# One set of rows for the sums of squares, one fixed zeroed tile of probabilities, and another buffer for a block's third result tile

## The chip, the cores and the metric

The kernel runs on one core of a Trainium2 chip. The metric is device microseconds of one execution. A core has five engines with queues of their own: TensorE (PE, matmuls), VectorE (DVE), ScalarE (ACT), GpSimd (POOL) and SyncE (SP), which here only issues transfers. The engines wait for each other by semaphores; an instruction that has to wait holds up all that stands behind it in its queue.

## The reference

Three layers in a row, on 4 x 576 = 2304 tokens of 512 features, in float32. The first is attention with 8 heads of 64; four heads look at a window of 32 keys, four at every fourth of 128. The second is a gated layer with a norm ahead of it, the third a layer with a PReLU.

```
mask_plain = (rel >= 0) & (rel < window)                                        # heads 0..3
mask_dil = (rel >= 0) & (rel < window * dilation) & (rel % dilation == 0)       # heads 4..7
attn = softmax(where(mask, scale * q @ k.T, -1e9)) @ v            # 4 x 8 x 576 x 64
x = attn as 2304 x 512
xn = x / sqrt(mean(x * x) + 1e-06) * rms_g
g = xn @ w_gate;  x = (g * sigmoid(g) * (xn @ w_val)) @ w_out     # 512 -> 1536 -> 512
h = x @ w_in;  out = (max(h, 0) + alpha * min(h, 0)) @ w_out      # 512 -> 2048 -> 512
```

## The kernel before

Every value that goes into a matmul is split into two float16 numbers, a high and a low part, and a product takes three matmuls (high-high, high-low, low-high). So most values are made twice: ACT writes the high part with a scale, DVE or POOL subtracts it from the value and writes the low part.

The tokens go through the two wide layers in seven blocks: 256, 256, 384, 384, 384, 256 and 384 tokens (blocks 0 to 6). A block has a phase A (`mm1`, `mm2`: the gated layer, closed by `y_out`) and a phase B (`mm3`, `mm4`: the PReLU layer, closed by `o_out`). Blocks 4 to 6 do phase B in a tail of their own. Each phase runs over chunks of 128 hidden features, and each chunk is a slot: the matmuls of the chunk, on ACT a Tanh (L921) or a Relu (L985) that evacuates PSUM, on DVE a second step (L922, L986), on ACT the high half (L925, L988), on POOL the low half (L931), and two slots later the matmuls that add the chunk to the result in PSUM (`acc`).

The attention is cut into groups of up to 96 queries x 128 keys x 4 heads. Its steps stand in a list, and between two slots some are taken from it, at a pace that has each block's tokens ready in time; each is given a high priority. The first groups use a path with float32 matmuls; the last 33 of them (the later path, some 224 to 690 us) use functions whose names begin with `a_`:

- `a_load` brings q into a tile `rq` and k and v into `rkv` (two buffers each), on SP's queue.
- `a_max` lets ACT square q, k and v (L511, three instructions) and add them up by row into `ams`. Of `ams` there were two sets, by `i % 2`, for each of three numbers of query rows (96, 64, 32).
- `a_split_hi` takes a ones matmul over these rows (`psw<-ams,ones`), DVE makes scales `sc` of it, and ACT writes the high halves of q, k and v (L537, L539, L540); `a_split_lo` adds the low halves.
- `a_turn_qk` transposes q and k by a transfer (L561, SP's queue) into `qkT`.
- `a_score` has the score matmuls, the softmax (four exponentials on ACT, L587), and writes the high half of the probabilities into `phl` (L700). Where a group has fewer than 128 keys, POOL first zeroes the other columns (L699). `a_prob` adds the low half (L706, POOL).
- `a_turn_p` transposes `phl` by a transfer (L712) into `pT`; `a_value` has the matmuls with v; `weigh` divides, by way of a tile `xd` of the tag `st` for dilated groups (L602 on ACT, L603 on DVE), and writes to DRAM.

Group i's steps are spread over neighbouring steps of the list: `a_max` of i stands in the list before the split of i, and the split of i - 1 before the `a_max` of i.

`o_tile` copies 128 tokens of a block's result out of PSUM into a tile `o` (L1003) and sends it out from ACT's queue (L1008). A block of 384 tokens has three. The tag `st` has two buffers, and `xd` uses it as well. The tag `hl2` has two buffers and holds the split rows: `yhl` of `y_out`, and `xhl` of the attention's norm.

The order of the instructions on each engine is not that of the code alone: the framework's scheduler orders them by dependencies, priorities and its own estimate of times. So a change of a buffer moves instructions elsewhere.

Of the kernel before, what the change touches and what calls it, by code (L numbers as in the profile page):

```python
# [8 lines left out]
F32 = mybir.dt.float32  # L9
F16 = mybir.dt.float16  # L10
# [19 lines left out]
def kernel(  # L30
# [14 lines left out]
    nc = tc.nc  # L45
    B, H, S, D = q.shape
    DM = H * D
# [3 lines left out]
    HH = H // 2  # L51
# [9 lines left out]
    wk = ctx.enter_context(tc.tile_pool(name="wk", bufs=1))  # L61
    dram = ctx.enter_context(tc.tile_pool(name="dram", bufs=1, space=DRAM))
    at_stack, ps_stack = ctx.enter_context(ExitStack()), ctx.enter_context(ExitStack())
    at = at_stack.enter_context(tc.tile_pool(name="at", bufs=1))
# [25 lines left out]
    vhl = [at.tile([128, HH, 2, D], F16, tag=f"vhl{i}", name=f"vhl{i}") for i in range(NV)]  # L90
    vh, vl = ([t[:, :, a] for t in vhl] for a in range(2))
    ams = const.tile([128, 3, 2, 3], F32, name="ams")
    scratch = dram.tile([B * S, HH * D], F32, name="scratch")

    def mm(o, a, b, start, stop):
        nc.tensor.matmul(o, a, b, start=start, stop=stop)  # L96

    def psw():
        return ps_w.tile([128, 512], F32, tag="w", name="psw")
# [17 lines left out]
    def band(m, rows, cols, c0, lo, hi, off=0, fill=-NEG):  # L117

        view = m[0:rows, c0:c0 + cols]
        nc.gpsimd.affine_select(  # L120
            out=view, in_=view, compare_op=ALU.is_ge, fill=fill,
            base=off - lo, pattern=[[1, cols]], channel_multiplier=-1,
        )
        nc.gpsimd.affine_select(
            out=view, in_=view, compare_op=ALU.is_ge, fill=fill,
            base=hi - off, pattern=[[-1, cols]], channel_multiplier=1,
        )

    def constants():
        nc.vector.memset(ident, 0.0)  # L130
        nc.gpsimd.affine_select(
            out=ident, in_=ident, compare_op=ALU.not_equal, fill=1.0,
            base=0, pattern=[[-1, 128]], channel_multiplier=1,
        )
        nc.vector.memset(ones_1, 1.0)
        nc.vector.memset(eps, 1e-30)
        nc.gpsimd.memset(qkhl, 0.0)
        nc.gpsimd.memset(ams, 0.0)
        nc.vector.memset(mhalf, -0.5)
        nc.vector.memset(m_spp, 0.0)  # L140
        for m in (m_norm, m_tail):
            nc.vector.memset(m, -BIG)
        band(m_spp, 128, 128, 0, -31, 0, fill=-BIG)

        et = wk.tile([4, 32, 4], BF16, tag="st", bufs=2, name="et")
        nc.vector.memset(et, 0.0)
        nc.gpsimd.affine_select(
            out=et, in_=et, compare_op=ALU.not_equal, fill=1.0,
            base=0, pattern=[[0, 32], [-1, 4]], channel_multiplier=1,
        )  # L150
        same = psw()[:, 0:128]
        mm(same, et.rearrange("p a c -> p (a c)"), et.rearrange("p a c -> p (a c)"), True, True)
        nc.vector.tensor_scalar(m_spd, same, BIG, -BIG, ALU.mult, ALU.add)
        band(m_spd, 128, 128, 0, -127, 0, fill=-BIG)
        band(m_norm, 96, 128, 0, 1, 32)
        for r in range(2):
            view = m_tail[:, 48 * r:48 * r + 48]
            band(m_tail, 32, 48, 48 * r, 1, 32, 16 * r)
            nc.gpsimd.affine_select(
                out=view, in_=view, compare_op=ALU.is_ge, fill=-NEG,  # L160
                base=-16 if r else 15, pattern=[[0, 48]], channel_multiplier=1 if r else -1,
            )
# [342 lines left out]
    def a_max(i):  # L505
        g = groups[i]
        nq, nk = g["nq"], g["nk"]
        am = ams[:, {96: 0, 64: 1, 32: 2}[nq], i % 2]
        junk = wk.tile([128, 512], BF16, tag="junk", bufs=1, name="junk")[:, 0:HH * D]
        for n, c, src in ((nq, 0, g["rq"][:nq]), (nk, 1, g["rkv"][:nk, 0]), (nk, 2, g["rkv"][:nk, 1])):  # L510
            nc.scalar.activation(  # L511
                junk[:n], src.rearrange("p h d -> p (h d)"), ACTF.Square, accum_out=am[:n, c:c + 1])
        g["am"] = am
# [49 lines left out]
    def softmax(g, scores, scale, masked=False):  # L563

        nq, nk = g["nq"], g["nk"]
        s = g["s"]
        sv = s[:nq, :, :nk]
        for ps, hs in () if masked else scores:
            n = len(range(HH)[hs])
            nc.vector.scalar_tensor_tensor(  # L570
                s[:nq, hs, :nk], ps[:nq, :, :nk], scale,
                g["mask"][:nq, :nk].unsqueeze(1).to_broadcast([nq, n, nk]), ALU.mult, ALU.max)
        mx = at.tile([128, 2, HH], F32, tag="mx", bufs=4, name="mx")
        if masked:
            for ps, hs in scores:
                nc.vector.tensor_reduce(mx[:nq, 0, hs], ps[:nq, :, :nk], axis=AX.X, op=ALU.max)
            nc.vector.tensor_scalar(mx[:nq, 1], mx[:nq, 0], -scale, None, ALU.mult)
        else:
            nc.vector.tensor_reduce(mx[:nq, 1], sv, axis=AX.X, op=ALU.min)  # L579
        g["dn"] = at.tile([128, HH, 1], F32, tag="dn", bufs=4, name="dn")  # L580
        for ps, hs in scores if masked else ():
            for n, h in enumerate(range(HH)[hs]):
                nc.scalar.activation(
                    s[:nq, h, :nk], ps[:nq, n, :nk], ACTF.Exp, bias=mx[:nq, 1, h:h + 1], scale=scale,
                    accum_out=g["dn"][:nq, h])
        for h in () if masked else range(HH):
            nc.scalar.activation(  # L587
                s[:nq, h, :nk], s[:nq, h, :nk], ACTF.Exp, bias=mx[:nq, 1, h:h + 1], scale=-1.0, accum_out=g["dn"][:nq, h])
# [96 lines left out]
    def a_score(i):  # L685
        g = groups[i]
        nq, nk = g["nq"], g["nk"]
        qT, kT = g["qT"], g["kT"]
        ps = psw().rearrange("p (h c) -> p h c", h=HH)
        for h in range(HH):  # L690
            mm(ps[:nq, h, :nk], qT[:, 2 * h, :nq], kT[:, h, :nk], True, False)
            mm(ps[:nq, h, :nk], qT[:, 2 * h + 1, :nq], kT[:, h, :nk], False, True)
        g["s"] = at.tile([128, HH, 128], F32, tag="s", name="s")
        softmax(g, [(ps, slice(0, HH))], g["sc"][:nq, 6:7])
        sv = g["s"][:nq, :, :nk]
        phl = at.tile([128, 2, HH, 128], F16, tag="phl", name="phl")
        g["phl"] = phl
        if nk < 128:
            nc.gpsimd.memset(phl[:nq, :, :, nk:128], 0.0)  # L699
        nc.scalar.activation(phl[:nq, 0, :, :nk], sv, ACTF.Copy)  # L700

    def a_prob(i):
# [121 lines left out]
    def score(i):  # L824
        a_score(i)
        a_prob(i)
# [9 lines left out]
    def second_half(i):  # L836
        some((score, i - 2), (a_turn_qk, i - 1), (a_max, i))
        if i < NG:
            next_load(i)
# [156 lines left out]
    def o_out(j):  # L996
        rc = ysc.pop(j)
        for n in range(ncols(j) // 128):
            o_tile(j, n, acc[n], rc[:, n:n + 1])

    def o_tile(j, n, src, rc, eng=nc.scalar):
        o = wk.tile([128, DM], F32, tag="st", bufs=2, name="o")
        nc.scalar.activation(o, src, ACTF.Copy, scale=rc)  # L1003
        col = 0
        for t0, m in blocks[j][0]:
            a, e = max(col, n * 128), min(col + m, (n + 1) * 128)
            if a < e:
                eng.dma_start(  # L1008
                    out=out[t0 + a - col:t0 + e - col, :], in_=o[a - n * 128:e - n * 128, :])
            col += m  # L1010
# [106 lines left out]
    def out_t(t):  # L1117
        p = tail["acc"]
        tl = tail["tl"]
        m1 = tl.tile([128, 1, 256], F32, tag="m1", bufs=1, name="m1o")  # L1120
        nc.scalar.activation(m1[:, 0], p[3][:, 0], ACTF.Copy)

        y = tl.tile([128, 7, 256], F32, tag="yb", bufs=1, name="yo")
        nc.vector.tensor_tensor(y[:, 0:5:4], p[0][:, 0:2], m1.to_broadcast([128, 2, 256]), ALU.add)
        nc.vector.tensor_tensor(y[:, 6], p[2][:, 0], y[:, 4], ALU.add)
        nc.vector.tensor_tensor(y[:, 2:4], p[1][:, 0:2], y[:, 6:7].to_broadcast([128, 2, 256]), ALU.add)
        nc.vector.tensor_tensor(y[:, 5], p[1][:, 1], y[:, 4], ALU.add)
        nc.vector.tensor_tensor(y[:, 1], p[2][:, 1], y[:, 5], ALU.add)
        yv = y.rearrange("p a c -> p (a c)")
        for n in (1, 0):  # L1130
            i = 2 * t + n
            o_tile(*tiles[i], yv[:, n * 512:(n + 1) * 512], rct[:, i:i + 1], nc.sync if n else nc.scalar)
# [120 lines left out]
    fill()  # L1253
    nc.sync.dma_start(out=al, in_=alpha.rearrange("(c p) -> p c", p=128))
    constants()

    first = max(n for n, s in enumerate(steps) if s[1] == 0) + 1
# [104 lines left out]
```

## Time and profile before

| | before |
|---|---|
| median of three runs | 974.19 us (973.42 to 974.59) |
| the profiled execution | 973.93 us, span 972.1 us |
| PE busy | 912.4 us (94% of the span) |
| DVE busy | 675.2 us (69%) |
| ACT busy | 550.4 us (57%) |
| POOL busy | 324.2 us (33%) |
| granted TensorE clock, mean | 0.974 |

The span runs from the first instruction to the last; 1.8 us of the profiled execution lie around it. Busy times are sums over the whole span, and the engines work at the same time: what counts is where the engine that ends last had to wait.

### The profile page before, as it was taken

How to read it: one execution, taken by the hardware profiler on the slowest of the kernel's cores; microseconds unless marked ns; L12 is line 12 of the kernel's file. 1: busy time of each engine (PE TensorE's matmuls, PEld its weight loads, DVE VectorE, ACT ScalarE, POOL GpSimd, SP SyncE). 2: the span in 40 equal slices, each digit the busy share in tenths (PEclk: the TensorE clock that was granted, in tenths of full speed). 3: DMA queues.
4: the chain of work that ended last, by engine and by line, in shares of the span. 5: the costliest groups of instructions: out<-in, count | busy, mean ns of one | idle time of the engine just before them, and what ended most of it. 6: DMA issues, size and time to landing. Idle time of an engine off the chain costs nothing.

```text
span 972.1 us, 18834 instructions
## 1 busy us (share of the span) xinstructions
PE 912.4 (94%) x6760; PEld 618.8 (64%) x6760; DVE 675.2 (69%) x1602; ACT 550.4 (57%) x1537; POOL 324.2 (33%) x333
## 2 busy tenths in 40 slices
PE   6559899999998999998999999999999999999997
PEld 3547667865555666554555554555775557889986
DVE  5999897998878666565565775545554836777674
ACT  3426587756899866666655776544434324344342
POOL 2313341231444544332232233323253622322221
PEclk9678899999999999999999999999999999999999
DMA  9992356455236455544435554232311002000000
GB/s 264 326 353 85 94 167 168 136 165 142 52 62 95 97 101 83 106 84 89 101 75 83 107 105 85 47 80 53 45 23 22 1 1 34 1 23 23 2 24 22
DMA packets 191614, 88.15 MB, mean 91 GB/s; under 512 B 176800, under 2 KB 180384, under 8 KB 191520
## 3 DMA queue, kind: packets, MB, share of 16 engines
q1 hardware_dynamic: 189504, 83.27, 37.4%
q10 hardware_dynamic: 2016, 3.67, 1.1%
q8 instruction: 53, 0.87, 0.4%
q14 instruction: 41, 0.34, 0.1%
HBM read 55.32 MB, written 6.55 MB: 64 GB/s over the span
## 4 chain that ended last, share of the span: by engine, by line
PE 54%; DVE 15%; DMA 11%; ACT 9%; issue 7%; POOL 2%; SPq 1%; ACTq 0%; DVEq 0%; POOLq 0%
PE psw L96 24%; PE p L96 15%; PE acc L96 14%; ACT s L587 2%; DMA rkv<-in_v_dram 2%; DMA rkv<-in_k_dram 2%; DVE wb L230 2%; DVE wb L231 2%; DMA wb<-in_moe_w_out_dram 2%; DMA rq<-in_q_dram 2%; DVE wb L407 1%; DVE wb L229 1%; ACT junk L511 1%; ACT wb L402 1%; DVE t L922 1%
## 5 line engine op out<-in xcount | busy, mean ns | idle before, releaser
L96 PEld LDWEIGHTS <-wb 128*128 128x128 f16 (+1 forms) x4866 | 454.0, 99 | 203.6 <-DVE wb L231 17.9
L96 PE MATMUL psw<-xyall,wb 128*128 128x384 f16 (+1 forms) x2784 | 431.2, 305 | 4.4 <-DVE xd L603 1.5
L96 PE MATMUL acc<-wb,hlall 128*128 128x512 f16 x822 | 198.7, 380 | 5.6 <-ACT hlall L988 2.3
L96 PEld LDWEIGHTS <-hlall 128*128 128x128 f16 x822 | 78.7, 98 | 89.3 <-POOL hlall L931 5.4
L931 POOL TENSOR_TENSOR hlall<-t,hlall 128x384 f16<-128x384 f32 (+1 forms) x58 | 59.3, 1022 | 160.3 <-ACT hlall L925 142.0
L96 PE MATMUL acc<-wb 128*128 128x512 f16 (+1 forms) x402 | 83.6, 353 | 18.7 <-DVE wb L231 15.5
L96 PE MATMUL p<-xyall,wb 128*128 128x256 f16 (+1 forms) x960 | 88.7, 251 | 0.0
L1096 POOL TENSOR_TENSOR wb<-fa,wb 128x640 f16<-128x640 f32 x32 | 45.4, 1421 | 111.8 <-ACT wb L1095 111.8
L922 DVE SCALAR_TENSOR_TENSOR t<-t,psw 128x384 f32<-128x384 f32 (+1 forms) x84 | 41.0, 489 | 53.0 <-ACT t L921 53.0
L96 PE MATMUL p<-wb 128*128 128x256 f16 x672 | 77.6, 273 | 0.3 <-DVE yhl L966 0.3
L921 ACT ACTIVATE t<-psw,tsc 128x384 f32<-128x384 f32 (+1 forms) x84 | 44.0, 524 | 40.9 <-PE psw L96 39.1
L587 ACT ACTIVATE s<-s,mx 96x128 f32<-96x128 f32 (+2 forms) x132 | 50.0, 380 | 15.3 <-DVE mx L579 13.8
L931 POOL TENSOR_TENSOR hlall<-p,hlall 128x256 f16<-128x256 f32 (+1 forms) x49 | 39.8, 814 | 56.3 <-ACT hlall L988 45.1
L986 DVE SCALAR_TENSOR_TENSOR p<-m,oma,psw 128x256 f32<-128x256 f32 (+1 forms) x64 | 34.5, 538 | 31.3 <-ACT m L985 30.9
L1094 DVE SCALAR_TENSOR_TENSOR wb<-fa,wb 128x384 f16<-128x384 f32 x32 | 40.5, 1269 | 22.2 <-ACT wb L1093 22.1
L402 ACT ACTIVATE wb<-wb,wsg 128x512 f16<-128x512 f32 x68 | 46.1, 711 | 16.8 <-DVE wsg L339 10.2
L706 POOL TENSOR_TENSOR phl<-s,phl 96x512 f16<-96x512 f32 (+2 forms) x33 | 36.0, 1090 | 58.4 <-ACT phl L700 50.5
L1095 ACT ACTIVATE wb<-fa 128x640 f16<-128x640 f32 x32 | 23.5, 735 | 55.9 <-DVE fa L1088 55.9
L405 POOL TENSOR_TENSOR wb<-wb 128x512 f16<-128x512 f32 x28 | 38.2, 1371 | 39.9 <-ACT wb L404 20.9
L231 DVE SCALAR_TENSOR_TENSOR wb<-wb 128x512 int32<-128x512 int32 (+1 forms) x56 | 49.8, 891 | 0.2
L594 DVE TENSOR_SCALAR dn<-dn 96x4 f32<-96x4 f32 (+3 forms) x52 | 8.4, 162 | 58.9 <-ACT s L587 53.7
L931 POOL TENSOR_TENSOR wb<-t,wb 128x256 f16<-128x256 f32 (+1 forms) x26 | 27.4, 1055 | 63.5 <-ACT wb L925 63.5
(202 smaller groups left out, 1383.3 us busy)
## 6 DMA issues: line engine op xcount, KB each, us to landing
wb<-in_moe_w_out_dram SPq DMA_DIRECT2D x28, 512.0 KB, 4.4
wb<-in_moe_w_in_dram SPq DMA_DIRECT2D x16, 512.0 KB, 3.8
wb<-in_moe_w_gate_dram SPq DMA_DIRECT2D x12, 512.0 KB, 6.7
wb<-in_moe_w_val_dram SPq DMA_DIRECT2D x12, 512.0 KB, 6.9
out_dram<-o ACTq DMA_DIRECT2D x14, 256.0 KB, 3.8
rkv<-in_k_dram SPq DMA_DIRECT2D x23, 128.0 KB, 2.5
rkv<-in_v_dram SPq DMA_DIRECT2D x23, 128.0 KB, 3.0
rq<-in_q_dram SPq DMA_DIRECT2D x23, 96.0 KB, 2.0
```

What stands on the lines that cost most here:

```text
L96: nc.tensor.matmul(o, a, b, start=start, stop=stop)
L231: nc.vector.scalar_tensor_tensor(w, r[:, :, :, 0], 29, w, ALU.logical_shift_right, ALU.bitwise_or)
L402: nc.scalar.activation(half(b, 0), dec(b), ACTF.Copy, scale=wsg[:, s:s + 1])
L405: nc.gpsimd.tensor_tensor(half(b, 1), dec(b), half(b, 0), ALU.subtract)
L587: nc.scalar.activation(s[:nq, h, :nk], s[:nq, h, :nk], ACTF.Exp, bias=mx[:nq, 1, h:h + 1], scale=-1.0, accum_out=g["dn"][:nq, h])
L706: nc.gpsimd.tensor_tensor(phl[:nq, 1, :, :nk], g["s"][:nq, :, :nk], phl[:nq, 0, :, :nk], ALU.subtract)
L921: nc.scalar.activation(t[:, :T], pg[:, :T], ACTF.Tanh, scale=tsc[:, chunk(c):chunk(c) + 1])
L922: nc.vector.scalar_tensor_tensor(t[:, :T], t[:, :T], 1.0, pg[:, :T], ALU.add, ALU.mult)
L931: nc.gpsimd.tensor_tensor(a[:, 1, :T], t[:, :T], a[:, 0, :T], ALU.subtract)
L986: nc.vector.scalar_tensor_tensor(p[:, :T], m[:, :T], oma[:, c:c + 1], ps[:, :T], ALU.mult, ALU.add)
L1094: nc.vector.scalar_tensor_tensor(l[:, 0:3], f[:, 0:3], 0.25, h[:, 0:3], ALU.mult, ALU.subtract)
L1096: nc.gpsimd.tensor_tensor(l[:, 3:8], f[:, 3:8], h[:, 3:8], ALU.subtract)
```

## The change

Three edits. The rows for the sums of squares have one set instead of two. The tile of probabilities `phl` is one tile for all groups, zeroed once at the start by POOL, instead of one allocated for each group with the unused columns zeroed each time. The third result tile of a block takes a buffer of the tag `hl2` instead of `st`.

```diff
+    phl = at.tile([128, 2, HH, 128], F16, tag="phl", name="phl")
...
         nc.gpsimd.memset(ams, 0.0)
+        nc.gpsimd.memset(phl, 0.0)
...
-        am = ams[:, {96: 0, 64: 1, 32: 2}[nq], i % 2]
+        am = ams[:, {96: 0, 64: 1, 32: 2}[nq], 0]
...
-        phl = at.tile([128, 2, HH, 128], F16, tag="phl", name="phl")
         g["phl"] = phl
-        if nk < 128:
-            nc.gpsimd.memset(phl[:nq, :, :, nk:128], 0.0)
         nc.scalar.activation(phl[:nq, 0, :, :nk], sv, ACTF.Copy)
...
     def o_tile(j, n, src, rc, eng=nc.scalar):
-        o = wk.tile([128, DM], F32, tag="st", bufs=2, name="o")
+        o = wk.tile([128, DM], F32, tag="hl2" if n == 2 else "st", bufs=2, name="o")
```

With the added lines the line numbers shift: L511 becomes L513, L537, L539 and L540 become L539, L541 and L542, L587 becomes L589, L602 becomes L604; behind `a_score` they are one lower (L700 becomes L699, L985 L984, L988 L987, L1003 L1002, L1008 L1007).

The instructions also change their order. On ACT, in block 2's phase B, the squares of one group (96 query rows) stood ahead of the exponentials of the group two before it; this is the place in the trace around 450 to 455 us. `wb` is a chunk's high half, `m` the Relu's result. Before:

```order
L988 ACTIVATE wb<-p 128x384
L511 ACTIVATE junk,ams<-rq 96x256
L511 ACTIVATE junk,ams<-rkv 128x256 x2
L587 ACTIVATE s,dn<-s,mx 96x128 x4
L985 ACTIVATE m<-psw 128x384
L700 ACTIVATE phl<-s 96x512
L988 ACTIVATE wb<-p 128x384
L537 ACTIVATE qkhl<-rq,sc 96x4x2x64
L539 ACTIVATE qkhl<-rkv,sc 128x4x64
L540 ACTIVATE vhl_86<-rkv,sc 128x4x64
```

The same place on ACT in the changed kernel:

```order
L987 ACTIVATE wb<-p 128x384
L589 ACTIVATE s,dn<-s,mx 96x128 x4
L984 ACTIVATE m<-psw 128x384
L699 ACTIVATE phl<-s 96x512
L513 ACTIVATE junk,ams<-rq 96x256
L987 ACTIVATE wb<-p 128x384
L513 ACTIVATE junk,ams<-rkv 128x256
L539 ACTIVATE qkhl<-rq,sc 96x4x2x64
L541 ACTIVATE qkhl<-rkv,sc 128x4x64
L542 ACTIVATE vhl_86<-rkv,sc 128x4x64
L513 ACTIVATE junk,ams<-rkv 128x256
```

The three squares have moved behind the exponentials, the Relu and the copy of the probabilities, to both sides of the split copies of the group before them.

The second place on ACT is the end of block 2, where its three result tiles are copied, around 463 to 470 us. Before:

```order
L921 ACTIVATE t<-psw,tsc 128x384
L1003 ACTIVATE o<-acc,rc 128x512 x2
L1008 DMA out_dram<-o 128x512
L587 ACTIVATE s,dn<-s,mx 96x128 x4
L1008 DMA out_dram<-o 128x512
L1003 ACTIVATE o<-acc,rc 128x512
L700 ACTIVATE phl<-s 96x512
L1008 DMA out_dram<-o 128x512
L602 ACTIVATE xd<-psw 32x256
```

And in the changed kernel:

```order
L920 ACTIVATE t<-psw,tsc 128x384
L1002 ACTIVATE o<-acc,rc 128x512 x2
L1007 DMA out_dram<-o 128x512
L589 ACTIVATE s,dn<-s,mx 96x128 x4
L1007 DMA out_dram<-o 128x512
L1002 ACTIVATE o<-acc,rc 128x512
L604 ACTIVATE xd<-psw 32x256
L699 ACTIVATE phl<-s 96x512
L1007 DMA out_dram<-o 128x512
```

The copy into `xd` has moved ahead of the copy of the probabilities and now comes right behind the third result tile.

The third place is on SP's queue, around 558 to 562 us, where the loads of one group and the transpose of q and k of another leave. Before:

```order
L608 DMA scratch<-xd 96x256
L499 DMA rq<-in_q_dram 96x4x64
L501 DMA rkv<-in_k_dram 128x4x64
L561 DMA_TRANSPOSE qkT<-qkhl 128x12x96
L503 DMA rkv<-in_v_dram 128x4x64
```

And in the changed kernel:

```order
L610 DMA scratch<-xd 96x256
L501 DMA rq<-in_q_dram 96x4x64
L503 DMA rkv<-in_k_dram 128x4x64
L505 DMA rkv<-in_v_dram 128x4x64
L563 DMA_TRANSPOSE qkT<-qkhl 128x12x96
```

The load of v has passed the transpose.

## Rows read from the trace of the kernel before

**Rows 1.** Busy time by stretch: PE, PEld, DVE, ACT, POOL; granted clock, DMA share, GB/s.

```profile
200.00:640.00 440.00, 422.42 (x2794) 248.52 (x2793) 298.74 (x763) 307.79 (x928) 159.98 (x172) 1.00 0.47 92
640.00:960.00 320.00, 319.74 (x2657) 239.86 (x2655) 197.16 (x446) 126.47 (x261) 107.18 (x96) 1.00 0.12 23
```

**Rows 2.** Line 511, the squares: ns min/median/max; idle time before them (us, times).

```profile
L511 ACT ACTIVATE junk<-rkv x66: 398/416/418, 224.2 to 636.9; 128x256 bf16<-128x256 f32 x46, 96x256 bf16<-96x256 f32 x20
...
  DMA rkv<-in_k_dram: 21.3, 19
  DMA rq<-in_q_dram: 21.1, 21
  DMA rkv<-in_v_dram: 7.0, 10
```

**Rows 3.** PE's timeline: start, us, instruction, idle before it and its releaser.

```profile
337.02 1.04 PE L96 MATMUL acc<-wb,hlall 128*128 128x512 f16 x4 [0.59 <-ACT hlall L988]
...
455.17 1.04 PE L96 MATMUL acc<-wb 128*128 128x512 f16 x4 [1.09 <-ACT wb L988]
...
496.82 0.97 PE L96 MATMUL psw<-xyall,wb 128*128 128x384 f16 x5 [0.34 <-DVE t L922]
...
531.76 0.44 PE L96 MATMUL psw<-qkT 128*96 128x128 f16 x5 [1.79 <-DVE t L922]
...
540.68 0.60 PE L96 MATMUL acc<-wb 128*128 128x512 f16 x2 [0.69 <-ACT wb L925]
...
572.31 0.52 PE L96 MATMUL psw<-vhl,pT 96*32 96x128 f16 x8 [0.54 <-DMA pT<-phl]
...
601.58 0.61 PE L96 MATMUL acc<-wb 128*128 128x512 f16 x2 [1.44 <-ACT wb L988]
```

**Rows 4.** ACT's timeline: two squares that waited for their load.

```profile
494.79 0.42 ACT L511 ACTIVATE junk<-rkv 128x256 bf16<-128x256 f32 x1 [0.81 <-DMA rkv<-in_v_dram]
...
530.14 0.42 ACT L511 ACTIVATE junk<-rkv 96x256 bf16<-96x256 f32 x1 [2.61 <-DMA rkv<-in_v_dram]
```

**Rows 5.** ACT's timeline: the copy that PE stood for at 455.17.

```profile
454.59 0.52 ACT L988 ACTIVATE wb<-p 128x384 f16<-128x384 f32 x1 [0.32 <-DVE p L986]
```

**Rows 6.** ACT's and PE's timelines: a third square, its read, the group's ones matmul.

```profile
574.03 0.40 ACT L511 ACTIVATE junk<-rkv 96x256 bf16<-96x256 f32 x1
574.33 0.19 ACT L511 ACTIVATION_READ_ACCUMULATOR junk<-rkv 96x1 f32 x1
...
578.49 0.18 PE L96 MATMUL psw<-ams,ones 96*128 96x3 bf16 x1
```

**Rows 7.** Line 503, issue of a v load; line 561, who waited for its transposes.

```profile
L503 SPq DMA_DIRECT2D rkv<-in_v_dram x39: 421/498/1776, 123.7 to 634.1; - x39
...
  PEld L96: 1.2, 2
  PE psw L96: 0.5, 1
```

**Rows 8.** ACT's and PE's timelines at the result tiles of block 2.

```profile
463.51 1.26 ACT L1003 ACTIVATE o<-acc,rc 128x512 f32<-128x512 f32 x2
...
468.42 0.69 ACT L1003 ACTIVATE o<-acc,rc 128x512 f32<-128x512 f32 x1 [1.95 <-DMA out_dram<-o]
...
469.52 0.37 ACT L602 ACTIVATE xd<-psw 32x256 f32<-32x256 f32 x1
...
470.39 2.11 PE L96 MATMUL psw<-xyall,wb 128*128 128x384 f16 x12 [1.47 <-DVE xd L603]
...
473.28 0.63 ACT L736 ACTIVATE xhl<-x 96x512 f32<-96x512 f32 x1 [2.25 <-DVE x L605]
```

**Rows 9.** Line 699, the memsets; their waits (us, times); line 137 by form.

```profile
L699 POOL MEMSET phl<- x10: 301/302/309, 298.7 to 689.6; 32x256 f16 x6, 64x256 f16 x4
...
  DMA pT<-phl: 22.7, 9
...
L137 POOL MEMSET qkhl<- 128x1536 f16 x1 | 1.4, 1377 | 0.3 <-POOLq L1340 0.3
```

## The prediction

> **What bounds the kernel now.** The first view is the table of stretches [rows 1]. From 200 to 640 us TensorE (PE) is busy 422.42 of 440 us at full granted clock; from 640 to 960 it is busy 319.74 of 320. So PE is the bound, and 17.6 us of holes between 200 and 640 are all that can be won after 200 us. Before 200 us the program keeps its order on every engine, but for one memset on POOL at the start. The later attention path, which the change touches, runs between 224 and 690 us.
>
> The second view is what the squares of `a_max` waited for [rows 2]. ScalarE (ACT) runs 99 of them (three for each of 33 groups) at 416 ns in the median, and stood 21.3, 21.1 and 7.0 us ahead of them until k, q or v had landed: 49.4 us. ACT has much idle time, so this costs only where something that PE needs stands behind a square on ACT's queue.
>
> The third view, PE's timeline, decides that. I took every hole of 0.3 us or more between 200 and 640 and followed it back: from the instruction that released PE to what that one waited for, until a wait for a load came or none was left. In seven places the way ends at a square that stood for its load [rows 3]; an eighth, at 292, begins at one too but has other waits on its way, and is left out. Two of these squares show the pattern [rows 4]: the one at 494.79 waited 0.81 us for v, the one at 530.14 waited 2.61. Behind it on ACT stand an evacuation of PSUM or the exponentials, then comes DVE, then PE's hole, 1 to 4 us later. The hole can be longer or shorter than the wait, since other work lies between.
>
> **The change, part by part.**
>
> *One set of rows.* With `i % 2` the squares of group i may run before the ones matmul of group i-1 has read its own row maxima; with index 0 they may not, if both have the same number of query rows. Nothing is computed more or less: 99 squares before and after. But the scheduler now puts them behind that matmul. Counting the other instructions ahead of each on ACT, 23 of the 33 groups have their first square 3 to 23 instructions later (10 in the median), most now close ahead of the split copies of the group before; nine stand where they stood, within one, and one comes earlier. The first place in the order on ACT shows it: before, the squares stood ahead of the exponentials of another group; now those run first. Ten instructions of at least the length of a square are 10 x 0.42 = 4.2 us that the load has more, an estimate from [rows 2], against single waits of 0.81 and 2.61 us [rows 4], so most of the waits go.
>
> Which holes close? Of the seven in [rows 3], five go back to a square that is moved: 0.59 (337.02), 1.09 (455.17), 0.34 (496.82), 0.69 (540.68) and 0.54 (572.31), together 3.25 us. The other two, 1.79 (531.76) and 1.44 (601.58), go back to groups that keep their place (the square at 530.14 is of one), and stay. Something else is late next where a hole closes: at 455.17 the copy L988 that releases PE had itself waited 0.32 us for DVE [rows 5], a third of that hole. I count a quarter of the 3.25 as coming back: -3.25 + 0.8 = -2.45 us.
>
> What it adds is a wait of the squares for the ones matmul, and behind them on ACT the copies that PE wants. The way from a square to the ones matmul of its own group tells how much room there is. The shortest among the moved groups is that of the group whose third square starts at 574.03 and whose matmul runs at 578.49 [rows 6]: 578.49 - 574.03 - 0.40 - 0.19 for the read of the sum = 3.9 us. Three squares take 3 x 0.416 = 1.2 us plus three such reads, 1.8 us in all, and the split copies have to wait for the scales from DVE anyway, so the squares fill time in which ACT would stand. Cost taken: 0; bound above: the rival below.
>
> The Trainium skill (Trainium Kernel Development and Optimization, Best Practices) says "Double-buffer for performance: Overlap DMA with compute". By that rule giving up the second set loses overlap, and the time would go up. The trace doesn't bear it out: what is doubled here is not the target of a transfer, and the second set only let ACT stand for loads sooner.
>
> *The order on SP.* The transposes of q and k (L561) leave from the same queue as the loads. Counting the loads ahead of each of the 33: seven have one or two more ahead of them now, two have one fewer. The order on SP shows one place: the v load passes the transpose. A v load holds the queue 0.50 us [rows 7], so at most 7 x 0.5 = 3.5 us if each transpose were waited for, and 0 if none. PE and its weight loads waited for such a transpose three times in 33 [rows 7]: 7 x 3/33 x 0.5 = 0.3 us. I take +0.3. The gain on the other side (the v load 1.5 us sooner, as long as a transpose holds the queue) is part of a rival.
>
> *The third result tile.* At 463.51 two copies of block 2's results fill both buffers of tag `st`; the third copy waits until the first transfer out has landed, and runs at 468.42 after 1.95 us of idle. Behind it stands `xd`, at 469.52, and PE, which had stood for it, goes on at 470.39 after 1.47 us [rows 8]. With its own buffer the third copy runs at once. But the next user of `st` is then `xd`, which waits for the same transfer: it can start where the copy started, at 468.42. Gain 469.52 - 468.42 = 1.10 us of the 1.47. Its bounds are 0 (if `xd` is late for another reason) and 1.47. The buffer taken from `hl2` is next wanted by an `xhl`; the first after it, at 473.28, takes the other buffer and waits for DVE anyway [rows 8]: 0. The other block with three tiles, block 3, ends past 640 us, where PE is full [rows 1], as it is at the two third tiles of the tail: 0.
>
> *The fixed zeroed tile.* Ten memsets of 0.30 us go from GpSimd (POOL), and with them 22.7 us in nine waits for the transpose before [rows 9]. No hole of PE goes back to one, and the longest waits lie past 640 us, where PE is full: 0. The low half of the probabilities, which POOL makes next, waits for the same transpose either way. The new memset at the start is 128 x 1024; the nearest row is 128 x 1536 in 1.38 us [rows 9], so about 0.92 us on POOL in the first microseconds, where PE waits for the q and k loads. 0, at most +0.9.
>
> **Sum.** -2.45 + 0.3 - 1.10 = -3.25 us against the profiled 973.93, that is 970.7. The median of the three runs is 0.26 above the profiled one; with it 970.9 us. About 0.2% (1.95 us) is what measurement can tell from no change, so this is faster by more than that, 0.33%, not by much.
>
> **Rivals.**
>
> *The wait changes owner.* The squares stand for the ones matmul instead of the load, and holes of the same size open at other places; the change then does only the 1.10: 973.1 us, no change by the bound. For it: the order of 23 groups shifts, and a hole's origin moves easily. Against it: 3.9 us of room where 1.8 are needed.
>
> *PE stands for the late squares: slower.* Where ACT reaches the squares late, the ones matmul, which stands in PE's queue among the large matmuls, waits, and PE with it. The mean of the seven holes is 6.48 / 7 = 0.93 us. Against the sum of -3.25, 3.25 / 0.93 = 3.5 such holes cancel the gain, and (3.25 + 1.95) / 0.93 = 5.6 make the kernel slower by 0.2%; one in every third of the 23 moved groups, seven, gives 970.9 + 7 x 0.93 = 977.4 us. Against it: no wait of PE for a square stands among the holes before. For it: the squares now come at the last place where they are in time.
>
> *The unmoved holes close too: faster still.* The sooner v loads and the shorter ACT queue ahead also shorten the waits of 1.79 and 1.44 us [rows 3], and nothing comes back: 973.93 - 3.25 - 3.23 - 1.10 + 0.26 = 966.6 us.
>
> **How the numbers follow.** Forecast as reckoned 0.48; unmoved holes too 0.14; owner changes 0.26; slower 0.12. So faster 0.62, same 0.26, slower 0.12. The likeliest case alone spans 969.5 to 972.5: all five holes, 1.47 for the tile and 0 for SP, 973.93 - 3.25 - 1.47 + 0.26; or half of them, 1.10 and 1 us for SP, 973.93 - 1.63 - 1.10 + 1.0 + 0.26. For 8 in 10 the range takes in the rival at 966.6 and of the slower one the part near no change: 966.6 to 976.0.
>
> **What would show it.** Right: ACT's idle time ahead of the squares falls from 49.4 us to about 10; PE's busy time from 200 to 640 stays 422 while that stretch's work ends about 3 us sooner, with the five holes gone; ahead of the third result tile no wait, `xd` behind it waits about 2 us for the transfer out; the memsets of the probabilities gone and nothing else changed by it; PE's holes before 200 us as they were. Wrong: PE waits for a square ahead of the ones matmul, or new holes of 0.5 us and more behind the transposes of q and k.

## The result and the profile after

The changed kernel takes 958.78 us in the median of four runs (957.45 to 959.12), against 974.39 (973.42 to 975.72) for the one before: ratio 0.9836, 95% interval 0.9819 to 0.9853. That is 15.6 us, almost five times the forecast of 3.25, and outside the range. The profiled execution has a span of 956.9 us.

The busy time by stretch of the changed kernel, in the columns of [rows 1]:

```profile
200.00:640.00 440.00, 433.28 (x2890) 257.90 (x2888) 299.38 (x784) 313.69 (x949) 159.95 (x169) 1.00 0.48 95
640.00:940.00 300.00, 300.00 (x2529) 227.81 (x2527) 185.34 (x419) 117.12 (x238) 101.78 (x89) 1.00 0.11 20
```

PE now stands 6.7 us of the 440, not 17.6; past 640 us it is full, as before. What the squares waited for (line 513 now):

```profile
its engine sat idle before it (us, times) until:
  DMA rq<-in_q_dram: 5.7, 6
  DMA rkv<-in_k_dram: 4.3, 3
  DMA rkv<-in_v_dram: 2.9, 3
  PE psw L97: 0.3, 1
```

So 12.9 us of load waits are left of the 49.4 in [rows 2], in 12 places instead of 50; the wait for the ones matmul, which takes their place, is 0.3 us in one.

PE's timeline, all holes of at least 0.2 us that are left between 255 and 680 us:

```profile
292.08 1.25 PE L97 MATMUL acc<-wb,hlall 128*128 128x512 f16 x5 [1.10 <-ACT hlall L924]
...
300.41 0.55 PE L97 MATMUL psw<-vhl,pT 128*96 128x128 f16 x8 [1.51 <-DVE sg L340]
...
342.96 0.82 PE L97 MATMUL acc<-wb,hlall 128*128 128x512 f16 x3 [0.56 <-ACT hlall L987]
...
547.14 0.59 PE L97 MATMUL psw<-vhl,pT 128*96 128x128 f16 x8 [0.45 <-DMA pT<-phl]
```

The kernel before had 21 such holes in this stretch, 14.7 us together. The third of the four that are left, 0.56 us at 342.96, stands where the kernel before had none. All seven of [rows 3] are closed, the two of groups that keep their place among them. At one of these two groups ACT still waits for its loads, as its timeline shows:

```profile
507.92 0.42 ACT L513 ACTIVATE junk<-rq 32x256 bf16<-32x256 f32 x1 [0.85 <-DMA rq<-in_q_dram]
...
511.38 0.42 ACT L513 ACTIVATE junk<-rkv 96x256 bf16<-96x256 f32 x1 [2.50 <-DMA rkv<-in_k_dram]
...
515.61 0.42 ACT L513 ACTIVATE junk<-rkv 96x256 bf16<-96x256 f32 x1 [1.24 <-DMA rkv<-in_v_dram]
```

These are the squares of the group that had the wait of 2.61 us in [rows 4]: 4.6 us of waits stand here, and no hole of PE follows.

The third result tile of block 2, on ACT:

```profile
457.72 0.67 ACT L1002 ACTIVATE o<-acc,rc 128x512 f32<-128x512 f32 x1
458.88 0.37 ACT L604 ACTIVATE xd<-psw 32x256 f32<-32x256 f32 x1 [0.50 <-DMA out_dram<-o]
```

The copy runs at once, and `xd` behind it waits 0.50 us for the transfer out.

Where the 15.2 us between the two profiled executions come from, by stage: I paired the 3,744 matmuls that read `xyall` (each one's place in the order of its kind is the same in both) and took the difference of their start times. At 47 us the changed kernel is 2.4 us behind, at 245 us 1.3. Between 245 and 257 us 1.7 come back, which is the clock: from 240 to 250 us the execution before had a granted clock of 0.83, this one 1.00. From 257 to 605 us it goes from 0.4 ahead to 14.8; past that only 0.4 is added. So 14.4 us come from the stretch of the later attention path: 3.0 of them up to 450 us, 4.9 between 450 and 473, 1.1 between 473 and 504, 3.0 between 525 and 548, and 2.3 between 548 and 605.

Not all of the 14.4 can be put down to the change. The hole of 1.47 us at the third result tile is 0.45 us at most in the profiles of the kernels below, and those of 0.28 us at 479 and of 0.34 at 497 behind it are in none; together they are 2.1 us. In the execution before, the first transfer out (issued at 464.22) landed after 4.11 us. In the profiles with the second edit alone, with one group moved and with three, which change little or nothing of the order up to there, it landed after 2.0 to 2.4 us, and the third copy didn't wait for it. With one group moved that copy is

```profile
465.12 0.67 ACT L1003 ACTIVATE o<-acc,rc 128x512 f32<-128x512 f32 x1
```

Why the transfer took longer in that one execution is not shown.

### The profile page after: what moved, and what is told of

Same layout as the page of the kernel before. It is cut to its first block, busy times and chain, and to the rows that moved or that the text cites. A ratio compares the mean times of both kernels' runs of the same rounds, so it can differ in the third digit from the quotient of the medians.

```text
span 956.9 us, 18827 instructions
## 1 busy us (share of the span) xinstructions
PE 906.7 (95%) x6760; PEld 619.6 (65%) x6760; DVE 666.4 (70%) x1602; ACT 548.2 (57%) x1537; POOL 321.2 (34%) x324
## 4 chain that ended last, share of the span: by engine, by line
PE 74%; DVE 10%; DMA 6%; ACT 4%; issue 2%; SPq 2%; POOL 1%; DVEq 0%; ACTq 0%; POOLq 0%
PE psw L97 34%; PE acc L97 22%; PE p L97 16%; DMA wb<-in_moe_w_out_dram 2%; DVE wb L232 2%; DVE wb L233 2%; ACT wb L404 2%; DVE wb L231 1%; DVE wb L409 1%; SPq L212 1%; SPq L629 1%; DMA wb<-in_moe_w_val_dram 1%; DMA wb<-in_moe_w_gate_dram 1%; DMA wb<-in_q_dram 1%; PE psw L639 1%
## 5 line engine op out<-in xcount | busy, mean ns | idle before, releaser
L97 PE MATMUL psw<-xyall,wb 128*128 128x384 f16 (+1 forms) x2784 | 425.0, 303 | 2.1 <-DVE sqo L284 1.2
L921 DVE SCALAR_TENSOR_TENSOR t<-t,psw 128x384 f32<-128x384 f32 (+1 forms) x84 | 41.0, 488 | 47.0 <-ACT t L920 47.0
L589 ACT ACTIVATE s<-s,mx 96x128 f32<-96x128 f32 (+2 forms) x132 | 50.1, 381 | 23.4 <-DVE mx L581 21.1
L985 DVE SCALAR_TENSOR_TENSOR p<-m,oma,psw 128x256 f32<-128x256 f32 (+1 forms) x64 | 34.5, 540 | 24.4 <-ACT m L984 24.0
L922 DVE SCALAR_TENSOR_TENSOR t<-t,psw 128x384 f32<-128x384 f32 (+1 forms) x84 | 41.1, 489 | 12.1 <-PE psw L97 11.0
```

Source lines behind the costliest of these rows:

```text
L589: nc.scalar.activation(s[:nq, h, :nk], s[:nq, h, :nk], ACTF.Exp, bias=mx[:nq, 1, h:h + 1], scale=-1.0, accum_out=g["dn"][:nq, h])
L921: nc.vector.scalar_tensor_tensor(t[:, :T], t[:, :T], 1.0, pg[:, :T], ALU.add, ALU.mult)
L922: nc.vector.scalar_tensor_tensor(t[:, :T], t[:, :T], 2.0 ** -46, pv[:, :T], ALU.mult, ALU.mult)
```

## The experiments

**The three edits apart.** The first edit alone:

```diff
-        am = ams[:, {96: 0, 64: 1, 32: 2}[nq], i % 2]
+        am = ams[:, {96: 0, 64: 1, 32: 2}[nq], 0]
```

> Only the first edit: one set of rows for the sums of squares. Theory S (the squares that stood for their loads at the head of ScalarE's queue are the source of nearly all holes, the ones counted and those that follow from them): 959.5 to 962 us, the idle time ahead of the squares 49 to below 15 us, the holes of TensorE between 255 and 640 us gone but for four or five, the hole at the third result tile still there. Theory P (the memsets of the probabilities on GpSimd hold part of it): 964 to 969 us. Theory O (any new order on the queues gives a new time, with no mechanism in it): nothing definite, anywhere from 958 to 976.

957.55 us (956.51 to 957.92), ratio 0.9811, interval 0.9783 to 0.9840: the whole gain, and a little below theory S's numbers. PE is busy 434.45 of the 440 us from 200 to 640, the load waits ahead of the squares are 12.6 us, and three holes of at least 0.2 us are left between 255 and 680 us. The second edit alone:

> Only the second edit: the fixed zeroed tile of probabilities, no memsets on GpSimd later. Theory S: 973.5 to 975 us, as before, with 49 us of idle time ahead of the squares. Theory P: 5 to 10 us faster, 964 to 969 us, with the holes of TensorE that GpSimd released gone. Theory O: anywhere from 958 to 976.

973.96 us, ratio 0.9988 (0.9970 to 1.0007): nothing that can be told from no change, and theory P's 5 to 10 us are not there. The third alone:

> Only the third edit: the third result tile in a buffer of the split rows. Few instructions move. Theory S and theory P: the hole of 1.47 us after block 2's results closes or shrinks, 972.5 to 973.5 us. Theory O: 973 to 975, since the order hardly changes.

973.57 us, ratio 0.9964 (0.9944 to 0.9984). Faster, as forecast and perhaps a little more, though its profiled execution has the span of the one before, 972.1 us. In its trace 1.6 us are gained at the third result tile: paired with the kernel before it is 2.0 us behind at 463 us, 0.4 at 473, 2.1 ahead at 573 and 0.3 behind at 604. But the profiles of the second edit alone and of one and three groups moved gain 1.0 to 1.6 us there too, without this edit, so the place doesn't show what the edit does. Of the 2.3 us lost at the end, 0.9 are a longer hole (2.34 us at 600.43, 1.44 in [rows 3]); the rest goes with a granted clock of 0.66 from 600 to 605 us. The second and third together, with two sets of rows:

> The second and third edits without the first, so two sets of rows as before. Theory S: 972.5 to 974 us, all holes but that at the third result tile as before. Theory P: 963 to 968 us. Theory O: anywhere from 958 to 976.

972.90 us, ratio 0.9978 (0.9961 to 0.9996). Theory S holds, theory P falls. Theory O is not ruled out by these alone: the first edit is also the one that moves most.

The trace of the first edit alone has a reading that the prediction's sum can't explain. It leaves the third tile's wait for the transfer where it was, but PE has no hole there; theory S, too, had expected that hole to stay. Its ACT and its PE at that place:

```profile
457.58 0.69 ACT L1003 ACTIVATE o<-acc,rc 128x512 f32<-128x512 f32 x1 [1.58 <-DMA out_dram<-o]
...
458.69 0.37 ACT L602 ACTIVATE xd<-psw 32x256 f32<-32x256 f32 x1
```

```profile
454.19 4.06 PE L96 MATMUL psw<-xyall,wb 128*128 128x384 f16 x24
458.09 0.55 PE L96 MATMUL psw<-vhl,pT 128*96 128x128 f16 x8
458.48 0.65 PE L96 MATMUL psw<-xyall,wb 128*128 128x384 f16 x3
458.97 0.17 PE L96 MATMUL psw<-ams,ones 128*128 128x3 bf16 x1
459.00 2.27 PE L96 MATMUL psw<-xyall,wb 128*128 128x384 f16 x13
```

PE goes on without a pause through the time in which ACT waits 1.58 us; in [rows 8] a wait of 1.95 us at the same place cost it 1.47.

**The wait or the place.** Is it the standing for loads that costs (W), or that 1.8 us of squares stood ahead of other work (R)? The next kernel has the first edit, and three readers of one column that stand for the loads in the old place:

```diff
+        tap = wk.tile([128, 4], F32, tag="tap", bufs=1, name="tap")
+        for n, c, src in ((nq, 0, g["rq"][:nq]), (nk, 1, g["rkv"][:nk, 0]), (nk, 2, g["rkv"][:nk, 1])):
+            nc.scalar.activation(tap[:n, c:c + 1], src.rearrange("p h d -> p (h d)")[:, 0:1], ACTF.Copy)
```

> The first edit alone (one set of rows), with three instructions of one column added for each group that read q, k and v on ScalarE as soon as they may; they take the place in the queue that the squares had, the squares stay late. Theory W (what costs is that ScalarE stands for a load with work of TensorE's behind it): the wait is back, 30 to 50 us of idle time ahead of these readers, and the time goes back to 968 to 975 us. Theory R (what costs is the length of the squares' own work, 1.8 us of each group, ahead of the exponentials): the squares are still late, 957.5 to 961 us, the difference being the added instructions.

977.32 us, ratio 1.0022 (1.0002 to 1.0041): the whole gain is gone, and a little more than theory W had said. For 31 of the 33 groups the readers stand within eight instructions of the squares' old place; those of the first two come far ahead of it, at 128 and 132 us. What its ACT waited for ahead of the readers (line 512):

```profile
its engine sat idle before it (us, times) until:
  DMA rq<-in_q_dram: 29.2, 27
  DMA rkv<-in_k_dram: 25.7, 20
  DMA rkv<-in_v_dram: 11.5, 16
```

That is 66.4 us, more than in [rows 2], and in the stretch from 200 to 640 us PE is busy 419.68 us. Paired with the kernel before, it is 3.0 us behind at 257 us and 5.35 at 605, so it loses 2.3 us where the first edit alone gains 15.2 (2.2 of the 2.3 around 605 us: a hole 0.7 us longer, and a granted clock of 0.66 from 605 to 610). The 99 readers take 0.20 us each, 20 us of ACT's time, which is not told apart from the wait here; the next kernel does that from the other side. It has two sets, and its squares wait for no load, since they read the norm's weights instead of q, k and v, so the scales are not those of the data:

```diff
-                junk[:n], src.rearrange("p h d -> p (h d)"), ACTF.Square, accum_out=am[:n, c:c + 1])
+                junk[:n], gs[:n, 0:HH * D], ACTF.Square, accum_out=am[:n, c:c + 1])
```

> Two sets of rows as before, but the squares read a tile that is there from the start (the norm's weights) instead of q, k and v, so that the scales are not those of the data and the results are not the reference's. The squares stand earlier on ScalarE's queue than before and wait for no load. Theory W: 955 to 961 us, as with one set. Theory R: the work still stands ahead of the exponentials of some group, 968 to 975 us.

960.51 us, ratio 0.9841 (0.9807 to 0.9875): the gain without the change. All its squares but those of the first three groups stand earlier than before, not later, take 0.40 us, and ACT waits 0.3 us ahead of them in all:

```profile
L511 ACT ACTIVATE junk<-gs x99: 398/404/418, 224.1 to 611.1; 128x256 bf16<-128x256 f32 x46, 96x256 bf16<-96x256 f32 x43, 32x256 bf16<-32x256 f32 x6, 64x256 bf16<-64x256 f32 x4
...
  PE psw L96: 0.3, 1
```

Theory R falls, and theory O with it, as two quite different orders give the same time and a third with the squares in their new place gives the old one. It is the waiting. (In this kernel the scales, too, no longer depend on a load; that this adds nothing is not shown by it, but the first edit alone has the gain without it.)

**Hole by hole, or on from one to the next.** One group alone, the one of the first place in the order on ACT:

```diff
-        am = ams[:, {96: 0, 64: 1, 32: 2}[nq], i % 2]
+        am = ams[:, {96: 0, 64: 1, 32: 2}[nq], (i - (i >= 37)) % 2]
```

> Two sets of rows, but one single group (the one whose squares stood at 449 to 452 us) has to use the set of the group ahead of it; its squares move behind the exponentials as in the changed kernel, and hardly anything else moves. Theory H (hole by hole, as in the prediction): the hole of 1.09 us at 455 closes and no other, TensorE gains 1.1 to 1.3 us on the kernel before between 450 and 480 us. Theory C (a late ScalarE makes the ones matmul, the scales and the next copies late, so that holes follow from holes): those of 1.27 and 0.38 us at 460 and 461 close as well, 3 to 3.5 us; if the reserve lasts to the third result tile, 4.5 to 5.

One run, 971.28 us, too few to judge a few us by; the trace can be paired. The hole at 455 closes, but the next two stay, and the first of them grows (PE's timeline):

```profile
460.30 0.60 PE L96 MATMUL acc<-wb,hlall 128*128 128x512 f16 x2 [1.86 <-ACT hlall L988]
461.29 1.04 PE L96 MATMUL acc<-wb,hlall 128*128 128x512 f16 x4 [0.38 <-POOL hlall L931]
...
467.62 3.41 PE L96 MATMUL psw<-xyall,wb 128*128 128x384 f16 x20
...
529.08 0.61 PE L96 MATMUL psw<-qkT 128*96 128x128 f16 x8 [1.87 <-DVE t L922]
```

At 463 us 0.7 us are gained (0.83 behind at 450, 0.16 behind now), less than by theory H. In the kernel before, PE's hole at 460 and ACT's work ahead of it were

```profile
460.14 0.60 PE L96 MATMUL acc<-wb,hlall 128*128 128x512 f16 x2 [1.27 <-ACT hlall L988]
```

```profile
459.57 0.52 ACT L988 ACTIVATE hlall<-p 128x384 f16<-128x384 f32 x1 [0.83 <-DVE p L986]
460.11 0.42 ACT L511 ACTIVATE junk<-rq 96x256 bf16<-96x256 f32 x1
```

and with the one group moved ACT's are

```profile
459.33 0.42 ACT L511 ACTIVATE junk<-rq 96x256 bf16<-96x256 f32 x1 [0.98 <-DMA rq<-in_q_dram]
...
459.74 0.51 ACT L988 ACTIVATE hlall<-p 128x384 f16<-128x384 f32 x1
```

The square of the next group now comes one instruction earlier, ahead of the copy that PE wants, and stands 0.98 us for its load: another load wait took up part of the gain. Then the hole at the third result tile, 1.47 us in [rows 8], is gone, and by 483 us 2.8 are gained; the holes near 479 and 497 are gone as well, 3.6 by 515. But these are the three holes that the profiles of the other kernels don't have either (0.45 us of the first at most), so their absence can't be put down to the moved group. At 532 the old hole stands, as do those at 541, 572 and 602, and 3.0 are still there at 605. What the moved group is shown to give is the 0.7 us: less than theory H, and the holes at 460 and 461 that theory C closes stay.

Three groups ahead of one that doesn't move:

```diff
-        am = ams[:, {96: 0, 64: 1, 32: 2}[nq], i % 2]
+        am = ams[:, {96: 0, 64: 1, 32: 2}[nq], (i - min(max(i - 38, 0), 3)) % 2]
```

> Two sets of rows, but three groups in a row (squares at 478 to 510 us) use the set of the group ahead. The group after them, whose squares wait 0.74, 2.65 and 2.61 us for their loads just before the hole of 1.79 us at 532, stays where it is. Theory H: the hole of 0.34 us at 497 closes, that at 532 stays at 1.5 to 1.9 us; 0.3 to 0.6 us gained. Theory C: ScalarE has made up time until then and the hole at 532 shrinks below 0.6 us or closes; 1.8 to 2.6 us gained.

One run, 973.33 us. PE's timeline has no hole between 520 and 541 us: that of 1.79 us and also that of 0.69 at 540 [rows 3] are closed, although the group there still waits 0.94, 2.32 and 1.89 us for its loads. Both holes stand in the profile of the kernel before and in those of the five other kernels that kept about its time (1.04 to 1.87 and 0.69 to 0.97 us). Between 483 and 548 us 3.75 us are gained, more than theory C said, 3.0 of them between 525 and 548. Half of it is lost again at 599:

```profile
599.41 3.26 PE L96 MATMUL acc<-wb 128*128 128x512 f16 x9 [1.86 <-ACT wb L988]
```

This hole is 0.4 us longer than in [rows 3], and from 600 to 605 us the granted clock is 0.66: 1.9 us lost between 594 and 604.

**Half of the waits.** The early readers again, but for every other group:

```diff
-        for n, c, src in ((nq, 0, g["rq"][:nq]), (nk, 1, g["rkv"][:nk, 0]), (nk, 2, g["rkv"][:nk, 1])):
+        for n, c, src in ((nq, 0, g["rq"][:nq]), (nk, 1, g["rkv"][:nk, 0]), (nk, 2, g["rkv"][:nk, 1])) if i % 2 else ():
             nc.scalar.activation(tap[:n, c:c + 1], src.rearrange("p h d -> p (h d)")[:, 0:1], ACTF.Copy)
```

> As the kernel with the early readers of one column and one set of rows, but with readers only for every other group, so half of the waits are put back. Theory L (each us of waiting costs the same wherever it stands): half way between 957.6 and 977.3, 966 to 969 us. Theory Q (a wait costs only when the groups ahead have left no reserve; single waits are absorbed): below 963 us.

960.24 us, ratio 0.9850 (0.9831 to 0.9868). What ACT waited for, from the list of waits (us in total, times, longest):

```profile
ACT tap L512 <- DMA rq<-in_q_dram: 14.2, 12, 2.0
...
ACT tap L512 <- DMA rkv<-in_k_dram: 12.3, 12, 2.9
...
ACT tap L512 <- DMA rkv<-in_v_dram: 5.7, 9, 1.7
...
ACT junk L514 <- DMA rkv<-in_k_dram: 5.3, 5, 2.5
...
ACT junk L514 <- DMA rq<-in_q_dram: 2.9, 4, 1.0
...
ACT junk L514 <- DMA rkv<-in_v_dram: 1.6, 1, 1.6
```

32.2 us of waits at the readers, half of 66.4, cost 960.24 - 957.55 = 2.7 us (the two intervals overlap); the other half cost 17. Theory L falls, and theory Q's number holds. That waits grow dearer the more there are is not shown by it alone: readers for the other groups only were not run, and their places may be the dearer ones. Nor is it the total that counts. With the squares' own 9.8 us, 42.0 us of load waits stand here, and almost the whole gain is kept; with three groups moved 40.4 us are left (line 511), and 21 holes of 14.9 us together between 255 and 680 us. What makes the same total cheap in one order and dear in the other is not shown.

**What is left of the waits.** All groups in one set, whatever their rows:

```diff
-        am = ams[:, {96: 0, 64: 1, 32: 2}[nq], 0]
+        am = ams[:, 0, 0]
```

> One set of rows for all groups whatever their number of query rows, without the other kinds' sets, on top of the first edit; the row maxima of a smaller group then include older rows of a larger one, so scales are a little lower. The groups that kept their place, with 10 us of waits left, are now held behind the ones matmul as well. Theory L: 2 to 4 us faster than one set for each kind, 954 to 956. Theory Q: those waits are already absorbed, 956.5 to 959 us.

955.15 us (954.91 to 957.65), ratio 0.9805 (0.9782 to 0.9828). The median lies in theory L's numbers, but the interval holds both. The load waits are down to 2.2 us. By the paired traces, the 9 us of waits between 380 and 590 us that went gave nothing, as theory Q has it, since there was no hole left there; 1.9 us come from between 287 and 350 us, where the first edit alone still has holes of 0.80, 1.50 and 0.57 us and this kernel only one of 1.05 and one of 0.22. It has the lowest median of all, but its interval overlaps those of the changed kernel and of the first edit alone.

**The third result tile beside the first edit.**

> The first and third edits. If the third result tile's buffer still pays beside the first edit: 956 to 956.8 us. If TensorE has reserve there anyway (the hole at this place is closed by the first edit alone, though the third copy still waits 1.58 us): 957 to 959 us, as the first edit alone.

958.95 us, ratio 0.9837 (0.9813 to 0.9860): as the first edit alone or with all three. In the paired traces both kernels gain the same 5.4 us between 450 and 483 us. The edit that is worth a little by itself shows nothing here.

## Why the prediction was wrong

The mechanism was the right one: squares that stood at the head of ACT's queue for their loads. So were the signs of the parts, and these sizes: idle time ahead of the squares down to 12.9 us (forecast about 10), no cost from the wait for the ones matmul, nothing that can be told from the memsets, the new memset 0.951 us (0.92). What failed is the step "Which holes close?" and the share that was taken back from it.

*Which holes close.* The step counted the five holes whose way back ended at the wait of a moved square, 3.25 us. In fact their number fell from 21 to four (three of the 21, that of 0.34 at 496.82 among them, are of the one execution), and the two unmoved ones of [rows 3] went with the others. A way back names the last cause of a hole: the instruction that was late. It does not tell why there was no ready work in PE's queue to bridge it. A load wait need not cost PE anything when ACT has a lead. The early readers for half of the groups show waits that cost little (2.7 us for 32), the three groups ahead of an unmoved one show that a lead is handed on (waits of 2.32 and 1.89 us left in place, hole closed), and the first edit alone shows a wait of 1.58 us at the third result tile with no hole behind it. What goes with the time is how long ACT waited for PE, that is, stood with all else done. In the list of waits of the changed kernel that row (the evacuation in phase A) is

```profile
ACT t L920 <- PE psw L97: 50.1, 32, 4.9
```

and before the change

```profile
ACT t L921 <- PE psw L96: 39.1, 26, 4.9
```

In the seven profiles of about the old time this row has 39.1 to 44.1 us, in the six fast ones 47.1 to 51.7. That goes with the result; that the change could have been priced from the row before it is not shown.

*The share taken back.* "Something else is late next where a hole closes" led to a quarter of the 3.25 being taken off. For the next hole it was right: with one group moved, that at 460 grew by 0.6 us, and 0.7 us were left of 1.09. With three groups moved it was wrong in sign: the holes behind an unmoved group closed too, 3.0 us. For all 23 groups a correction upward was called for.

*The sum.* A hole also costs more than the idle time which the timeline gives: the matmul of 384 columns ahead of that at 455.17 starts at 453.76, 1.41 us earlier; in the row ahead of it such matmuls start every 0.16 us, so 1.25 us are lost where the timeline gives 1.09. An estimate that takes this 0.16 for every hole: with 17 holes fewer that is 17 x 0.16 = 2.7 us beside the 14.7 - 3.6 = 11.1 of idle time; both together are 13.8 of the 14.4 us. The bound of 17.6 us for all that could be won was too low for the same reason.

*The third tile.* The step gave 1.10 us, with bounds 0 and 1.47, from a hole that had its 1.47 us in one execution alone, behind a transfer of 4.11 us; where it landed after 2.0 to 2.4 the hole is gone or at most 0.45 us without the edit. `xd` waits 0.50 us for the transfer in the changed kernel, where I had expected about 2. The third edit alone makes the kernel 0.16 to 0.56% faster by its interval; beside the first it shows nothing. The term was added to the sum as if it didn't hang on the first edit.

*SP's order.* The +0.3 us for the transposes didn't show: no hole for `qkT` of 0.2 us is left, one of 0.45 for `pT` is.

*The rivals.* The third one, the unmoved holes closing too, is what happened, with a chance of 0.14 and a price of 966.6 us; it was priced by those two holes alone. "The wait changes owner" fell (0.3 us of waiting for the ones matmul). "PE stands for the late squares" did not come: no hole of PE was released by a square. The Trainium skill's sentence that spoke against the edit (Trainium Kernel Development and Optimization, Best Practices: "Double-buffer for performance") does not hold for this second set: the first edit alone gives a ratio of 0.9811.

*What stays open.* Which waits PE's work can bridge, and why 42.0 us of them cost little in one order while 40.4 keep most holes open in another. That the changed kernel is 1.1 us behind from 120 to 240 us is unexplained; the new memset is not shown to be the cause, since the kernel with the second edit alone was 0.4 behind at 47 us, and that with the first alone, without the memset, 1.2. The order before 200 us is not quite the old one, either: in the kernels with the new memset, instructions on DVE and POOL around 5 us (the mask `m_spd`) have changed places with neighbours.

## What to carry to other kernels

When a queue in front of the bounding engine waits often and the holes it causes look small, don't price the waits by those holes one by one, nor by their total: behind the three moved groups waits of about 2 us cost nothing, and moving 23 groups closed holes that were traced to none of them. Take one row of one trace for a cost only after a second execution of the same order shows it: the hole of 1.47 us didn't come again. A buffer less can be faster, when the buffer's only use is to let an instruction that may have to wait get to the head of an in-order queue; test it by putting a one-column reader back in the old place. Two terms that may draw on the same lead shouldn't be added before they are tried together.

## What the runs showed of the hardware

PE's granted clock fell for a few us after some holes and not after others of much the same length. From 240 to 250 us it was 0.83 in the kernel before, after holes of 0.58 and 0.74 us, and in that with the third edit alone, after 0.96 and 0.74; in the changed kernel it was 1.00, after 0.77 and 0.74. Such a fall is worth 1.7 us, and the order of instructions up to there is the same but for a few at the start. One profile of the same order can so differ from another by 1.7 us. The stretch from 600 to 605 us at 0.66 in the kernel with three groups moved is of the same kind: matmuls of 512 columns that otherwise start every 0.21 us started every 0.43 us, half speed, 1.2 GHz instead of 2.4. And in the twelve other profiles the first 47 us, whose order on the queues is the same but for the new memset and a few neighbours of it, took between 0.1 us less and 2.8 us more than in that of the kernel before, which is as much as many edits are worth.

The time from issue to landing of one and the same transfer, the first result tile of block 2, was 4.11 us in the kernel before and 2.03 to 2.51 in the five others with two sets of rows whose squares wait for loads; if the holes at 479 and 497 follow from it as well, that cost PE an estimated 2.6 us (three holes of 2.1 us, and 0.16 for each).
